# Windowed attention feeding a squared-ReLU MLP on one core: the first loads in another order, and the last quarter of W1 as two column halves

## The chip, the cores and the metric

The kernel runs on one core of one Trainium2 chip. The metric is the device time of one execution in microseconds (us). Three runs of the kernel before took 302.31, 302.37 and 302.68 us; the median is 302.37 us. Lower is better.

## What is computed

Eight batches of eight heads with 576 positions and 64 channels go through attention with a symmetric window of 32 positions. The result, laid out as 4608 tokens by 512 features, goes through a two-layer MLP.

```python
scores = (1/sqrt(64)) * q @ k^T              # per batch and head, 576 x 576
scores = where(|i - j| <= 32, scores, -1e9)
attn   = softmax(scores)
x      = (attn @ v) as [4608 tokens, 512]    # heads side by side
h      = x @ w_in                            # 512 -> 2048
out    = (relu(h) ** 2) @ w_out              # 2048 -> 512
```

Inputs and output are float32 in device memory; the products run in bf16 with float32 accumulation.

## The kernel before, in words

**Groups.** A group G is 192 tokens of one batch: three per batch, 24 in all (G = 3·batch + g). For each group, K and Q are brought to SBUF and turned so that the head channels lie on the partitions (`turn_pe` for batches 0 and 1, `turn_dma` later). Then `scores` (S) makes two windows A and B with matmuls, ScalarE takes the exponential, VectorE masks it, `pv` (P) multiplies with V, VectorE normalises into `xa` and `xb`, and `xturn` (T) turns the result into XT, the MLP's input. For the first three groups T runs on TensorE, later by DMA from the SP queue.

**MLP.** `mm1` makes h^T for some tokens: it is called At0.d below (first token t0, first of two blocks d of 128 hidden columns; for the first 768 tokens it is 8 matmuls of 192 columns). ScalarE applies relu (line 758), VectorE squares into GT (line 761). Two PSUM banks ht0 and ht1 take turns, and four relu buffers. A0.0 and A0.2 read the first quarter of W1, A0.4 and A0.6 the second, A0.8 and A0.10 the third, A0.12 and A0.14 the last. `mm2` is called Bu.seg: 128 output tokens u, a quarter seg of the hidden columns, 4 matmuls of 512 columns; it reads quarter seg of W2.

**Order of the work.** Every step is recorded with its engine, what it reads and writes, a duration and a key. `schedule` (lines 129 to 232) plays this through with a cost table and places the step with the smallest key among those ready; `emit` then writes one fixed instruction list for each engine, with semaphore waits. At run time each engine takes its list in order: a step whose input is late holds up all that stand behind it on that engine. Where TensorE has a gap in the plan, idle matmuls on zeros are put in (line 324).

**First loads.** Nearly all loads are issued from GpSimd (POOL): they cast float32 to bf16 and go through one software queue, in the order of `OPENING` (lines 71 to 74). K and Q of group 0 are the exception: `load_hw` (line 400) loads them as float32 from SP into a staging tile `oe`, and ScalarE and VectorE cast them. Below, "k3" is K of group 3, "v2.1" the second V tile of group 2, "w1.3" the last quarter of W1. In bf16 a quarter of W1 or W2 has 512 KB, a Q load 192 KB, K 224, 192 or 160 KB (g = 0, 1, 2), a V tile 64 to 128 KB. The kernel's order is: q2, v0.1, v0.0, k1, v1.0, q1, **w1.0**, k2, **w1.1**, v1.1, **w1.2, w1.3**, v2.0, v2.1, w2.0, q3, k4, k3, v5.0, w2.1, v4.1, w2.2, v3.0, q4, v4.0, v3.1, w2.3, v5.1, k5, q5.

**Regrouping.** `load_pair` (line 424) loads K and Q of batches 0 and 1 with two neighbouring positions in one row. For G < `NRAWP` (groups 0 to 2) `turn_pe` turns these rows as they lie, with 16 transposes into 64 output partitions each (line 499). For groups 3 to 5 a VectorE copy (line 439) first regroups the rows, and 8 transposes into 128 output partitions follow (line 501).

**Gates on later loads.** From group 6 on a load waits for an earlier step (`gate`, line 383): before group `GFAR` for the score or MLP step recorded last, from it on for the second P step (PB) of the group three before.

Of the kernel before, what the change touches and what calls it, by code (L numbers as in the profile page):

```python
# [18 lines left out]
RING = 1536  # L19
NV, NRAW = 6, 6  # L20
NTURN = 2
NRAWP = 3
TCOL = 200
NXT = 3
LEAD = 13.0
LAG = 9.0
AHEAD = 9.0
GFAR = 9
GATE = 'P{}B'
GD = 3  # L30
GK = 8.5
# [3 lines left out]
HMOVE = 27  # L35
PMOVE = 20
WMOVE = 81
VMOVE = 14.5
TISS = 1340
TMOVE = 15  # L40
# [8 lines left out]
VCS = 6  # L49
NDUP = 1  # L50
NPR = 4
LSLACK1 = 1000
HOLD = {'PE': 300}
KMIN = 0.5
HOLDT = 26000
KSPL = 0
XTD = 1
# [10 lines left out]
VSET = (-12, -9)  # L68
ESPLIT = 0
IOTA = -1  # L70
OPENING = [("q", 2), ("v", 0, 1), ("v", 0, 0), ("k", 1), ("v", 1, 0), ("q", 1), ("w1", 0), ("hq", 0), ("k", 2), ("w1", 1), ("v",
           1, 1), ("w1", 2), ("w1", 3), ("v", 2, 0), ("v", 2, 1), ("w2", 0), ("q", 3), ("hk", 0), ("k", 4), ("k", 3), ("v", 5, 0),
           ("w2", 1), ("v", 4, 1), ("w2", 2), ("v", 3, 0), ("q", 4), ("v", 4, 0), ("v", 3, 1), ("w2", 3), ("v", 5, 1), ("k", 5),
           ("q", 5)]
WARM = 40000
LAST = ((0, 256), (256, 384), (384, 512))
KC = ((0, 224), (224, 192), (416, 160))
# [196 lines left out]
def act(n):  # L274
    return 175 + 0.833 * n


def dve(n, fast=True):
    return 153 + (0.52 if fast else 1.04) * n


class Gen:
# [100 lines left out]
    def gate(self, G):  # L383
        if G < 6:
            return None
        return self.p.named[GATE.format(G - GD)] if G >= GFAR else self.moe

# [36 lines left out]
    def load_pair(self, t, b, g, key):  # L424
# [5 lines left out]
        s = (self.q if t == "q" else self.k)[b][:, t0:t0 + n, :].rearrange("h (p r) d -> p h (r d)", r=2)  # L430
        if G < NRAWP:
            self.p.rec("POOL", lambda e: e.dma_start(self.pairs(raw)[0:h].rearrange("p (h c) -> p h c", c=128), s),  # L432
# [4 lines left out]
                   dma=(f"{t}p{G % NPR}", G), key=key, dur=500 + 3 * h, move=(h // 2, PMOVE), name=f"{t}{b}{g}",  # L437
                   slack=LSLACK1 if b else 0)
        self.p.rec("DVE", lambda e: e.tensor_copy(raw[0:h, :, :].rearrange("p r (h d) -> p r h d", d=64),
# [4 lines left out]
    def load_v(self, b, g, key, js=(0, 1)):  # L444
        G = 3 * b + g
        vt = self.V[G % NV]
        for j in js:
            k0 = 192 * g - 32 + 128 * j
            lo, hi = max(k0, 0), min(k0 + 128, S_)
            if g and j == 0 and G < NVR:  # L450
# [3 lines left out]
                vt[lo - k0:hi - k0, j, :, 0:64], self.v[b, :, lo:hi, :].rearrange("h p d -> p h d")),  # L454
                writes=[("v", G % NV, j)], dma=(f"v{G % NV}{j}", G), key=key, dur=500 + 3 * n, move=(n // 2, VMOVE),
                name=f"v{b}{g}{j}", after=self.gate(3 * b + g), slack=LSLACK if b > 1 else LSLACK1 * b)

# [3 lines left out]
                   reads=[("v", (G - 1) % NV, 1)], writes=[("vl", G % NV)], key=key + VKEY, dur=300, name=f"vc{G}",  # L461
                   after=self.moe if G >= VCS else None)

    def load_w1(self, d, key):
        src = self.w_in[:, 512 * d:512 * d + 512].rearrange("(f p) c -> p f c", p=128)
        self.p.rec("POOL", lambda e: e.dma_start(self.W1[:, :, 512 * d:512 * d + 512], src),  # L466
                   writes=[("w1", d)], dma=(f"w1{d}", 0), key=key, dur=770, move=(32, WMOVE), name=f"w1{d}")

    def load_w2(self, d, key):
        src = self.w_out[512 * d:512 * d + 512, :].rearrange("(k p) c -> p k c", p=128)  # L470
        self.p.rec("POOL", lambda e: e.dma_start(self.W2[:, 4 * d:4 * d + 4, :], src),
                   writes=[("w2", d)], dma=(f"w2{d}", 0), key=key, dur=770, move=(32, WMOVE), name=f"w2{d}")

# [8 lines left out]
    def turn_pe(self, t, b, g, key):  # L482
# [9 lines left out]
        def f(e):  # L492
            for j in range(4):
                for x in range(2):
                    c = n * j + h * x
                    if G < NRAWP:
                        for u in range(2):
# [6 lines left out]
        self.p.rec("PE", f, reads=[("raw", t, G % NRAW, 0), ("raw", t, G % NRAW, 1), "id"], writes=tag, key=key,  # L504
                   dur=8 * 52 + TCOL * (G < NRAWP), name=f"turn{t}{b}{g}")
        if G < NPAIR:
# [233 lines left out]
    def mm1(self, t0, n, ds, key):  # L740
        k = self.k1
        self.k1 += 1
        ht, rt, gt = self.HT[k % 2], self.RT[k % 4], self.GT
        r = t0 % RING
        c = n * len(ds)
        d0 = ds[0]
        steps = [(t0 // 64 + x) % (RING // 64) for x in range(n // 64)]

        def f(e):
            for x, d in enumerate(ds):  # L750
                for ft in range(4):
                    mm = e.matmul(ht[:, n * x:n * x + n], self.W1[:, ft, 128 * d:128 * d + 128], self.XT[:, ft, r:r + n],  # L752
                                  start=(ft == 0), stop=(ft == 3))
            return mm

        self.moe = self.p.rec("PE", f, reads=[("xt", s) for s in steps] + [(("xt", s), 1) for s in steps if t0 < 192 and XTD] + [("w1", d0 // 4)], writes=[f"ht{k % 2}"], key=key,
                   dur=4 * len(ds) * max(n / 2.4 + 2.5, 33), name=f"A{t0}.{d0}")
        self.p.rec("ACT", lambda e: e.activation(rt[:, 0:c], ht[:, 0:c], ACTF.Relu), reads=[f"ht{k % 2}"],  # L758
                   writes=[("rt", k % 4)], key=key, dur=act(c), name=f"r{t0}.{d0}")
        rr = rt[:, 0:c].rearrange("p (d t) -> p d t", d=len(ds))  # L760
        self.p.rec("DVE", lambda e: e.tensor_tensor(gt[:, d0:d0 + len(ds), r:r + n], rr, rr, ALU.mult),  # L761
                   reads=[("rt", k % 4)], writes=[("gt", s, d) for s in steps for d in ds], key=key, dur=dve(c),
                   name=f"g{t0}.{d0}")
# [50 lines left out]
    def build(self):  # L814
        p = self.p
        self.k1 = 0
        self.moe = None
        K = -100.0
        self.setup_idle()
        self.setup_iota(K + IOTA)  # L820
        self.setup_id(K)
        self.setup_mask(2, K + 1)
        self.setup_bias(2, K + 1.1)
        self.setup_mask(1, K + 2)
        self.setup_bias(1, K + 2.1)
        self.setup_k(0, K + 0.5)
        self.setup_v(0, K + 1.5)
        self.setup_v(1, VSET[0])
        self.setup_v(2, VSET[1])
        self.setup_mask(0, MKEY[0])  # L830
        self.setup_mask(3, MKEY[1])
        for i in range(3, NV):
            self.setup_v(i, -9)
        self.setup_k(1, -9)
        for n, it in enumerate(self.opening()):
            kd, a = it[0], it[1:]
            key = K + n
            if kd == "w1":
                self.load_w1(a[0], key)
            elif kd == "w2":  # L840
                self.load_w2(a[0], key)
            elif kd == "v":
                self.load_v(*divmod(a[0], 3), key, a[1:])
            elif kd[0] == "h":
                self.load_hw(kd[1], a[0], key)
            else:
                self.load_pair(kd, *divmod(a[0], 3), key)
        for g in (1, 2, 4, 5):
            self.copy_v(g, K + 7 if g < 3 else 3 * g - LEAD - AHEAD)
        todo = []  # L850

        def at(key, f, *a):
            todo.append((key, len(todo), f, a))

        for G in range(NG):
            b, g = divmod(G, 3)
            if b > 1:
                key = 3 * G - LEAD - (GK if G >= GFAR else AHEAD)
                for t in "kq":
                    at(key, self.load_pair if G < NPAIR else self.load_qk, t, b, g, key)  # L860
                at(key, self.load_v, b, g, key)
                if g and G < NVR:
                    key = 3 * G - LEAD - 0.5 if G >= VCS else key
                    at(key + 0.01, self.copy_v, G, key - VKEY if G >= VCS else key)
            for t in "kq":
                key = 3 * G - LEAD - (0.6 if b < NTURN else TDKEY)
                at(key, self.turn_pe if b < NTURN else self.turn_dma, t, b, g, key)
            for ws in ((0,), (1,)) if G < NSPLIT else ((0, 1),):
                at(3 * G - LEAD + 0.3 * ws[0], self.scores, G, ws)
            for w in range(2):  # L870
                at(3 * G - LEAD + 0.3 * w + 0.1, self.pv, G, w)
            at(3 * G - LEAD + 0.5, self.xturn, G)
        t0 = 0
        while t0 < NTOK:
            n = FIRST[t0] if t0 in FIRST else 192 if t0 < 768 else 256 if t0 < T512 else 512
            m = min(512 // n, 4)
            for d in range(0, 16, m):
                key = t0 / 64 + d / 16 * n / 64
                at(key, self.mm1, t0, n, list(range(d, d + m)), key)
            t0 += n  # L880
        at(500, self.mm2_last, NBLK - 1, 500)
        for u in range(NBLK - 1):
            for seg in range(4):
                at(2 * u + LAG + seg * 0.5, self.mm2, u, seg, 2 * u + LAG + seg * 0.5)
        for key, _, f, a in sorted(todo, key=lambda x: x[:2]):
            f(*a)
        p.schedule()
        with self.nc.Block():
            dsems, dcount = p.emit()
            for s in dsems:  # L890
                if s[0] == "o":
                    self.nc.sync.wait_ge(dsems[s], dcount[s])

    def opening(self):
        return OPENING

# [31 lines left out]
```

## Time and profile before

| | us |
|---|---|
| median of three runs | 302.37 |
| the profiled execution's own time | 302.63 |
| its span, first to last instruction | 300.5 |
| TensorE busy | 291.0 (97 %) |
| VectorE busy | 164.8 (55 %) |
| ScalarE busy | 160.6 (53 %) |
| GpSimd busy (all of it issuing loads) | 106.9 (36 %) |
| granted TensorE clock | 1.00 in every stretch |

The profile is of one execution. TensorE's share counts the idle matmuls as busy. The time of a load is given from its issue to its landing, when its semaphore lets a waiting engine go on; loads of one queue overlap, so the distance between two landings is what one of them adds. A program on one core has one granted clock, and here it is 1.00 throughout.

### The profile page before, as it was taken

The page shows a single profiled execution, that of the slowest core. Times are in us where ns is not written, and L with a number is a line of the kernel's source. Part 1 is how long each engine was busy: PE and PEld are TensorE (multiplying, and loading weights), DVE is VectorE, ACT ScalarE, POOL GpSimd, SP SyncE. Part 2 cuts the span into 40 slices and gives each one's busy share as a digit, 9 for nine tenths or more (in the row PEclk, how much of TensorE's full clock was granted, in tenths as well). Part 3 has the DMA queues.
Part 4 walks back from the last instruction along what each step waited for, and adds up shares of the span by engine and source line. Part 5 has one row for each costly group of instructions (what it writes and reads, how often), then busy time and mean ns, then how long its engine had stood idle before and what let it go on. Part 6 is the DMA issues. An engine that isn't in the chain of part 4 may idle for free.

```text
span 300.5 us, 6284 instructions
## 1 busy us (share of the span) xinstructions
PE 291.0 (97%) x2431; PEld 170.5 (57%) x2469; DVE 164.8 (55%) x381; ACT 160.6 (53%) x250; POOL 106.9 (36%) x143
## 2 busy tenths in 40 slices
PE   7888999999999999999999999999999999999997
PEld 2567885857767777754444444444544544444445
DVE  6787586666775757652765666546557632222100
ACT  3775555846656746650766376536646643443312
POOL 8992065235543661365246235533500000000000
DMA  9999999998999999999999999999992110001012
GB/s 162 191 199 185 192 180 197 182 163 131 158 182 146 113 157 142 171 127 169 180 158 85 154 165 150 139 146 161 160 130 65 55 52 37 35 35 37 36 70 105
DMA packets 160636, 39.83 MB, mean 133 GB/s; under 512 B 149984, under 2 KB 156128, under 8 KB 160608
## 3 DMA queue, kind: packets, MB, share of 16 engines
q0 software_dynamic: 106016, 17.93, 86.6%
q1 hardware_dynamic: 49264, 12.14, 28.0%
q10 hardware_dynamic: 5328, 9.37, 10.0%
q8 instruction: 19, 0.31, 0.4%
q14 instruction: 9, 0.07, 0.1%
HBM read 36.70 MB, written 9.44 MB: 154 GB/s over the span
## 4 chain that ended last, share of the span: by engine, by line
PE 90%; DMA 5%; POOL 3%; issue 1%; ACT 0%; POOLq 0%
PE ht L752 41%; PE outp L772 40%; DMA w<-in_moe_w_in_dram 5%; PE at L580 4%; PE at L637 4%; POOL v L453 1%; POOL w L466 1%; PE at L501 1%; PE ht L797 1%; PE outp L797 1%; POOL qraw L432 1%; POOL kraw L432 0%; ACT rt L758 0%; ACT oe L782 0%; ACT oe L807 0%
## 5 line engine op out<-in xcount | busy, mean ns | idle before, releaser
L752 PE MATMUL ht<-xt,w 128*128 128x256 bf16 (+2 forms) x885 | 140.0, 302 | 1.9 <-DMA w<-in_moe_w_in_dram 1.1
L772 PE MATMUL outp<-w,gt 128*128 128x512 bf16 x534 | 133.4, 379 | 1.5 <-issue 0.2
L758 ACT ACTIVATE rt<-ht 128x512 bf16<-128x512 f32 (+1 forms) x152 | 85.7, 578 | 80.0 <-PE ht L752 75.9
L752 PEld LDWEIGHTS ht<-xt,w 128*128 128x128 bf16 x896 | 81.1, 98 | 44.5 <-ACT rt L758 1.1
L761 DVE TENSOR_TENSOR gt<-rt 128x512 bf16<-128x512 bf16 (+1 forms) x152 | 61.5, 409 | 67.2 <-ACT rt L758 65.6
L772 PEld LDWEIGHTS outp<-w,gt 128*128 128x128 bf16 x560 | 52.0, 98 | 54.8 <-ACT oe L782 1.3
L396 POOL DMA_DIRECT2D kraw<-in_k_dram x36 | 27.7, 778 | 108.0 <-issue 43.6
L604 ACT ACTIVATE e<-at 128x1024 bf16<-128x1024 f32 x46 | 44.8, 1022 | 12.4 <-PE at L580 12.2
L609 DVE TENSOR_TENSOR pt<-e,mask 128x1024 bf16<-128x1024 bf16 x46 | 31.7, 692 | 26.8 <-ACT e L604 26.6
L782 ACT ACTIVATE oe<-outp 128x512 f32<-128x512 f32 x35 | 20.9, 599 | 36.1 <-PE outp L772 36.1
L453 POOL DMA_DIRECT2D v<-in_v_dram x48 | 38.4, 815 | 0.0
L396 POOL DMA_DIRECT2D qraw<-in_q_dram x36 | 27.8, 780 | 0.0
L637 PEld LDWEIGHTS at<-v,pt 128*128 128x128 bf16 x384 | 18.1, 98 | 10.6 <-issue 1.7
L637 PE MATMUL at<-v,pt 128*128 128x65 bf16 x384 | 20.1, 194 | 1.2 <-DVE at L665 1.0
L659 DVE TENSOR_TENSOR xa<-at,rs 64x512 bf16<-64x512 f32 x24 | 16.7, 694 | 0.8
L659 DVE TENSOR_TENSOR xb<-at,rs 128x512 bf16<-128x512 f32 x24 | 16.6, 690 | 0.8
L580 PEld LDWEIGHTS at<-qt,kt 64*128 64x128 bf16 x384 | 10.8, 94 | 9.4 <-issue 5.9
L580 PE MATMUL at<-qt,kt 64*128 64x128 bf16 x384 | 15.2, 218 | 0.7 <-ACT e L604 0.5
L656 DVE RECIPROCAL rs<-at 64x8 f32<-64x8 f32 (+1 forms) x48 | 10.0, 209 | 10.4 <-PE at L637 8.7
L665 DVE MEMSET at<- 64x520 f32 x23 | 11.3, 492 | 3.6 <-DVE xa L659 2.7
L804 DVE COPY oe<-ht 128x128 f32<-128x128 f32 x1 | 0.3, 292 | 14.7 <-PE ht L797 14.7
L460 DVE COPY v<-v 64x512 bf16<-64x512 bf16 x16 | 5.5, 346 | 4.3 <-PE ht L752 3.2
(69 smaller groups left out, 78.0 us busy)
## 6 DMA issues: line engine op xcount, KB each, us to landing
out_dram<-oe ACTq DMA_DIRECT2D x35, 256.0 KB, 3.0
qraw<-in_q_dram POOLq DMA_DIRECT2D x36, 96.0 KB, 5.4
v<-in_v_dram POOLq DMA_DIRECT2D x16, 128.0 KB, 7.0
w<-in_moe_w_in_dram POOLq DMA_DIRECT2D x4, 512.0 KB, 11.1
w<-in_moe_w_out_dram POOLq DMA_DIRECT2D x4, 512.0 KB, 18.9
v<-in_v_dram POOLq DMA_DIRECT2D x16, 96.0 KB, 6.0
kraw<-in_k_dram POOLq DMA_DIRECT2D x12, 112.0 KB, 4.6
kraw<-in_k_dram POOLq DMA_DIRECT2D x12, 96.0 KB, 5.5
```

The costliest lines, as they stand in the source:

```text
L396: self.p.rec("POOL", lambda e, j=j: e.dma_start(raw[0:h, j, :].rearrange("p (h d) -> p h d", h=8), s[:, j]), writes=[("raw", t, G % NRAW, ...
L453: self.p.rec("POOL", lambda e, j=j, lo=lo, hi=hi, k0=k0: e.dma_start(vt[lo - k0:hi - k0, j, :, 0:64], self.v[b, :, lo:hi, :].rearrange("h ...
L580: mm = e.matmul(sc[:, 512 * par + 128 * j:512 * par + 128 * j + 128], kt[r:r + 64, j, k0:k0 + 128], q, start=G >= NBIAS, stop=True, skip_g ...
L604: self.p.rec("ACT", lambda e, e_=e_, sc=sc: e.activation(e_[:], sc, ACTF.Exp, scale=0.125), reads=tags[w], writes=[("e", n % 2)], key=key, ...
L609: self.p.rec("DVE", lambda e, pt=pt, ee=ee, mb=mb: e.tensor_tensor(pt[:], ee, mb, ALU.mult), reads=[("e", n % 2), ("mask", mi)], writes=[( ...
L637: mm = e.matmul(avp[:, c:c + 65], pt[:, 4 * (h % 2) + h // 2, :], vt[:, w, h, 0:65], start=(w == 0 and y == 0), stop=True, skip_group_chec ...
L659: self.p.rec("DVE", lambda e: e.tensor_tensor(x[r0:128, :].rearrange("p (x y c) -> p x y c", x=2, y=4), av[:, :, :, 0:64], rb, ALU.mult), ...
L752: mm = e.matmul(ht[:, n * x:n * x + n], self.W1[:, ft, 128 * d:128 * d + 128], self.XT[:, ft, r:r + n], start=(ft == 0), stop=(ft == 3))
L758: self.p.rec("ACT", lambda e: e.activation(rt[:, 0:c], ht[:, 0:c], ACTF.Relu), reads=[f"ht{k % 2}"], writes=[("rt", k % 4)], key=key, dur= ...
L761: self.p.rec("DVE", lambda e: e.tensor_tensor(gt[:, d0:d0 + len(ds), r:r + n], rr, rr, ALU.mult), reads=[("rt", k % 4)], writes=[("gt", s, ...
L772: mm = e.matmul(op[:], gt[:, d, r:r + 128], self.W2[:, d, :], start=(d == 0), stop=(d == 15))
L782: self.p.rec("ACT", lambda e: e.activation(oe, op[:], ACTF.Copy), reads=[f"outp{u % 2}"], writes=[("oe", u % 4)], key=key, dur=act(512), n ...
```

## The change

The constants, the list of first loads, and two functions are changed; three numbers (`TCOL`, `WHALF`, `LSLACK1`) and `HOLD` only feed the planner's table, and so act through the order that it writes.

```diff
-NRAWP = 3
-TCOL = 200
+NRAWP = 4
+TCOL = 100
-GFAR = 9
+GFAR = 10
+WHALF = 43
-LSLACK1 = 1000
-HOLD = {'PE': 300}
+LSLACK1 = 500
+HOLD = {}
-OPENING = [("q", 2), ("v", 0, 1), ("v", 0, 0), ("k", 1), ("v", 1, 0), ("q", 1), ("w1", 0), ("hq", 0), ("k", 2), ("w1", 1), ("v",
-           1, 1), ("w1", 2), ("w1", 3), ("v", 2, 0), ("v", 2, 1), ("w2", 0), ("q", 3), ("hk", 0), ("k", 4), ("k", 3), ("v", 5, 0),
-           ("w2", 1), ("v", 4, 1), ("w2", 2), ("v", 3, 0), ("q", 4), ("v", 4, 0), ("v", 3, 1), ("w2", 3), ("v", 5, 1), ("k", 5),
-           ("q", 5)]
+OPENING = [("v", 0, 0), ("q", 1), ("k", 1), ("k", 2), ("v", 0, 1), ("v", 1, 0), ("hk", 0), ("v", 1, 1), ("q", 2), ("w1", 0),
+           ("w1", 1), ("w1", 2), ("w1", 3, 0), ("w1", 3, 1), ("v", 2, 0), ("v", 4, 0), ("q", 3), ("v", 2, 1), ("k", 3), ("q", 4),
+           ("k", 4), ("v", 3, 0), ("w2", 0), ("w2", 1), ("v", 3, 1), ("w2", 2), ("q", 5), ("v", 5, 1), ("w2", 3), ("k", 5), ("v",
+           4, 1), ("hq", 0), ("v", 5, 0)]
-    def load_w1(self, d, key):
-        src = self.w_in[:, 512 * d:512 * d + 512].rearrange("(f p) c -> p f c", p=128)
-        self.p.rec("POOL", lambda e: e.dma_start(self.W1[:, :, 512 * d:512 * d + 512], src),
-                   writes=[("w1", d)], dma=(f"w1{d}", 0), key=key, dur=770, move=(32, WMOVE), name=f"w1{d}")
+    def load_w1(self, d, key, half=None):
+        c, n = (512 * d, 512) if half is None else (512 * d + 256 * half, 256)
+        src = self.w_in[:, c:c + n].rearrange("(f p) c -> p f c", p=128)
+        self.p.rec("POOL", lambda e: e.dma_start(self.W1[:, :, c:c + n], src),
+                   writes=[("w1", d, x) for x in ((0, 1) if half is None else (half,))], dma=(f"w1{c}", 0), key=key, dur=770,
+                   move=(32, WMOVE if half is None else WHALF), name=f"w1{d}" + ("" if half is None else f".{half}"))
...
-        self.moe = self.p.rec("PE", f, reads=[("xt", s) for s in steps] + [(("xt", s), 1) for s in steps if t0 < 192 and XTD] + [("w1", d0 // 4)], writes=[f"ht{k % 2}"], key=key,
+        self.moe = self.p.rec("PE", f, reads=[("xt", s) for s in steps] + [(("xt", s), 1) for s in steps if t0 < 192 and XTD] + [("w1", d0 // 4, x) for x in sorted({d // 2 % 2 for d in ds})], writes=[f"ht{k % 2}"], key=key,
```

What it does to the written lists, read from the two programs:

- **POOL.** Ahead of W1 stand now v0.0, q1, k1, k2, v0.1, v1.0, v1.1, q2; these are the same eight loads that stood ahead of w1.3 before, two of them (k2, v1.1) formerly between the quarters. Then w1.0, w1.1, w1.2 and the two halves w1.3a, w1.3b. After them: v2.0, v4.0, q3, v2.1, k3, q4, k4, v3.0, **w2.0, w2.1**, v3.1, **w2.2**, q5, v5.1, **w2.3**, k5, v4.1, v5.0. So w2.0 has eight loads between itself and W1, where it had two.
- **SP.** The staged K of group 0 is issued first and Q second; before, Q was first.
- **TensorE.** A0.12 waits for w1.3a alone and A0.14 for w1.3b alone. Ahead of A0.12 stand the same steps as before; P2A (V of group 2) stands behind A0.14 now, where it stood between the two. From there the list runs P2A, two A, turn q3, A, P2B, A, turn k3, A, T2, A, T2, two A, S3, two A, B0.0, P3A, B1.0, two A, B0.1, P3B, two A, B0.2, turns k4 and q4, two A, S4, B1.1, B0.3. Over the whole program it has the same instructions, but for 32 transposes of group 3 in place of 16 and one more idle matmul. The last 45 steps are the same.
- **VectorE.** The two regrouping copies of group 3 are gone.
- **ScalarE.** The copy of the first two feature blocks of XT for group 0 (line 700) stands behind the exponential of S1B, where it stood ahead of it.

More of the change, by code (lines that the diff above doesn't have):

```diff
@@ L838, in build @@
             if kd == "w1":
-                self.load_w1(a[0], key)
+                self.load_w1(a[0], key, *a[1:])
             elif kd == "w2":
```

## The prediction, made before the changed kernel had run

> **What bounds the kernel now.** I read the page first: TensorE (PE) is busy nearly all the time, and the chain that ended last is PE but for one DMA.
>
> ```profile
> PE 291.0 (97%) x2431; PEld 170.5 (57%) x2469; DVE 164.8 (55%) x381; ACT 160.6 (53%) x250; POOL 106.9 (36%) x143
> ...
> PE   7888999999999999999999999999999999999997
> ...
> PE 90%; DMA 5%; POOL 3%; issue 1%; ACT 0%; POOLq 0%
> ```
>
> PE is below nine tenths only in the first four slices (30 us) and the last. Then the chain of the first 50 us in order of time, which names the DMA:
>
> ```profile
> 8.48 0.89 POOL v L453
> 9.37 0.71 POOL w L466
> 10.08 14.15 DMA w<-in_moe_w_in_dram
> 24.23 0.14 issue
> 24.36 0.82 PE ht L752 x8
> 25.18 0.25 PE at L637 x8
> ```
>
> The load issued at 10.08 is w1.3, landing at 24.23. The TensorE timeline (start, length, operation, idle before it) shows who waits:
>
> ```profile
> 13.49 0.53 PE L499 MATMUL ht<-ident,qraw 96*64 96x96 bf16 x16
> ...
> 21.44 0.82 PE L752 MATMUL ht<-xt,w 128*128 128x192 bf16 x8 [0.19 <-DMA w<-in_moe_w_in_dram]
> ...
> 22.65 0.82 PE L752 MATMUL ht<-xt,w 128*128 128x192 bf16 x8
> 24.36 0.82 PE L752 MATMUL ht<-xt,w 128*128 128x192 bf16 x8 [0.89 <-DMA w<-in_moe_w_in_dram]
> ...
> 31.11 0.51 PE L501 MATMUL at<-ident,qraw 96*128 96x96 bf16 x8
> ```
>
> A0.8 starts at 21.44, when w1.2 has landed (21.33), and A0.12 at 24.36, after 0.89 us of idling for w1.3. From there on PE runs through: the table by stages has it 49.6 of 50 us busy between 50 and 100, and no wait after 26 us is longer than 0.2. So **the span is 24.36 us plus the PE work behind the gate, 276.1 us**. An edit counts if it moves the gate, moves work across it, adds PE work behind it, or opens a new gap there.
>
> **1. Landing of the last part of W1.** Landings, from the loads' issue rows (issue plus time to landing): q2 7.70, k1 10.15, q1 11.46, w1.0 13.82, k2 14.68, w1.1 17.90, v1.1 18.76, w1.2 21.33, w1.3 24.23. Is this issuing or moving? The table of one-microsecond stretches:
>
> ```profile
> 7.00:8.00 1.00, 0.53 (x17) 0.45 (x18) 0.81 (x8) 1.00 (x2) 1.00 (x2) 1.00 2.34 157
> 11.00:12.00 1.00, 1.00 (x26) 0.67 (x26) 0.96 (x2) 0.77 (x1) 1.00 (x2) 1.00 1.26 211
> 45.00:46.00 1.00, 0.94 (x14) 0.64 (x12) 0.88 (x2) 0.81 (x2) 0.00 (x0) 1.00 2.41 162
> ```
>
> The last two columns are the DMA share, over 1 throughout, and GB/s: 157 with K, Q, V alone, 211 with W1 alone. The engines are full, so the order matters little and the bytes ahead decide. Ahead of the end of W1 stand the same eight loads, four quarters and two staged loads as before. GpSimd needs 0.75 to 0.9 us per issue, so w1.3b is issued near 10.6, over 12 us ahead of its landing. Hence w1.2 lands at 21.3 again, w1.3a halfway, at 22.8, and w1.3b at 24.2 plus what shorter runs cost. Halves write runs of 512 B, quarters 1 KB; the trace has no 512 B runs. Bounds for 512 KB: 0, at the quarters' 211 GB/s; 0.8, at the 157 of K, Q, V (3.3 us against 2.5). Nearest are quarters with runs twice as long, so I take **+0.1: w1.3b at 24.3**. An earlier landing is also possible (rival 1).
>
> The Trainium skill ("DMA: Bandwidth & Descriptors", Specifications) has full rate from 512 B upwards, by which this term would be 0 and the sum 0.1 lower; no run here has such a load.
>
> **2. Work moved across the gate.** Ahead of it stand the same steps, plus A0.12, which needs w1.3a only. Eight 192-column matmuls take 0.66 us in the chain (16 in 1.32). In the old order A0.10 is done by 23.4, and w1.3a comes before that, so A0.12 fits before 24.3 and **0.66 us leave the tail**. What covers it: the opening must be 0.7 us ahead of the gate. It is rearranged: the copy L700 stands behind the exponential of S1B. By the rows (exponential 1.02, query copy 1.03) ScalarE does S1A's exponential, q2's copy, S1B's exponential, then L700 until about 17.0, against 14.9 before; A0.0 starts near 17.1, not 15.75. Then A0.0, A0.2, P1B, S2B, A0.4, A0.6 and T1 take 0.66 four times, 0.26, 0.33 and 0.42, to 20.8 with about 0.6 of waits: ahead of w1.2's 21.3. If the opening were 1 us later still, the gain would shrink by what exceeds the 0.7.
>
> **3. Group 3 without regrouping.** 16 transposes replace 8. In the chain, 8 take 0.34 (q) and 0.39 (k); 16 of the L499 kind take 0.46 (96 columns, 11.51 to 11.97, when the next starts) and 0.52 (112). So **+0.25 on PE**. The two VectorE copies (0.42 each) were not on the path: gain 0.
>
> **4. Loads behind W1.** These are new waits on PE, and all steps stand behind them. From 24.3 I add the distances between landings that like loads had before (V tiles 0.4 to 0.75, Q 1.15, k3 1.26, k4 1.07, a W2 quarter 2.6), and walk PE through its list with chain durations (A 0.66, B 0.86, P 0.26, S 0.55, T 0.22):
>
> | load | lands | PE is there |
> |---|---|---|
> | v2.0 | 24.7 | 25.1 |
> | q3 | 26.35 | 26.7 |
> | k3 | 28.15 | 28.7 |
> | w2.0 | 33.55 | 34.2 |
> | w2.1 | 36.15 | 37.5 |
> | w2.2 | 39.5 | 39.95 |
> | w2.3 | 43.8 | 44.2 |
>
> All in time, but by 0.35 to 0.65 in most rows; before, w2.0 landed at 27.47 for a B0.0 at 29.26. I take 0; rival 2 has the other end. Other covers: the evacuation of k3 waits on VectorE behind the regrouping of q4 (lands 29.4), but S3 is not due before 32.3. The first MLP step on DMA-turned tokens (A576.0, near 47.9) needs T3: issued near 39.6, 6.7 to landing as now, 46.3.
>
> **5. Smaller edits.** K before Q on SP: the two staged loads share 832 KB and end at 6.79 either way; S0 starts within 0.3 of its 9.39, which part 2's slack covers. The later gate of group 9 and the planner's constants only reorder a tail of the same steps; a switch between kinds of matmul shows up to 0.1 (16 A in 1.43 instead of 1.32 after S), and their number is 269 against 266: 0, with 0.3 either way.
>
> **Sum:** −0.66 + 0.25 + 0.1 = −0.31 us. The profiled execution took 302.63 (span 300.5 and 2.1 around it); it becomes 302.3, span 300.2. That execution is 0.26 above the median, so the forecast against 302.37 is **302.05 us**. A measurement of this kernel tells about 0.2 %, 0.6 us, from no change: my forecast lies inside.
>
> **Rivals.**
> - **1. W1 lands earlier.** Speaks for it: w1.1 came 3.2 and w1.3 2.9 us after the load ahead, while a quarter alone at 211 GB/s takes 2.5. If K, Q, V are through at 13.1 (1152 KB, at the pace that brought 864 KB by 11.46) and the W1 loads then follow at 2.55, w1.3b is there at 23.3. Against: the excess is that engines already move the next load (v2.0 and v2.1 land 0.4 and 0.8 after w1.3), which is not lost. PE would reach A0.14 at 23.5: −0.66 − 0.8 + 0.25 = −1.2, **301.2**. Chance 0.2.
> - **2. Slower: W2 comes late.** Eight loads now stand between W1 and w2.0, and w2.3's margin is 0.4 over 19.5 us of stream, so a stream 2 % slower than reckoned decides it. Mechanism: S3 and so T3 come earlier (near 32 and 36.6, not 36.3 and 41.8), and SP's transposing DMAs fall among w2.2 and w2.3; with them the rate falls to 162 (the last row above). At 173 GB/s, the mean of 41 to 46, the 3584 KB from v2.0 to w2.3 take 21.2 us, w2.3 lands 1.3 after PE gets there: **303.4**. Against: w2.3 itself came in 2.5 us beside the first of these. Chance 0.22.
> - **3. The split does nothing**, the opening being so late that A0.12 starts when w1.3b is there: −0.66 is gone, +0.35 stays, **302.7**. Chance 0.1.
> - **4. The second half pays a fixed time of its own.** v1.0 (64 KB) landed 0.46 after its forerunner and needs 0.39 at 167 GB/s, so a load adds 0.1 at most beyond its bytes: 302.15, inside the forecast, and its chance of more is 0.03. The Trainium skill ("DMA: Bandwidth & Descriptors", Anatomy of one DMA) has a fixed 2 us per DMA, mostly the receipt; were it paid in series, w1.3b would land 2 us late, 1.6 above the forecast. By that page, as by the trace, such times overlap where loads are queued.
>
> **Chances.** Forecast 0.45, own range 301.5 to 302.6 (parts 2 and 5 give 0.3 either way, part 1 up to 0.7 more): 0.12 of it beyond the 0.6 on the fast side, 0.33 within. Rival 1: 0.2, faster. Rival 2: 0.22, of which 0.03 within. Rivals 3 and 4: 0.13, 0.11 within. Faster 0.32, same 0.47, slower 0.21. Range: rival 1's time to most of rival 2's: 301.2 to 303.1.
>
> **What would show it.** Part 1: w1.3b landing between 24.1 and 24.6. Part 2: an A step running while w1.3b is in flight, and PE idle for a DMA once more ahead of A0.14. Part 3: L499 with 32 more matmuls near 27 and 29 us. Part 4: no PE wait for a DMA after that gate; a gap ahead of the first B on w2.0, w2.2 or w2.3, or of a turn of group 3, proves it wrong. A gate below 23.8 is rival 1. An idle stretch after 100 us that I did not name would be a failure of part 5.

## The result, and the profile after

The changed kernel took 304.43 us (median of six executions, 303.66 to 305.37); the kernel before, measured beside it, 302.52 (six, 302.25 to 303.46). The ratio is **1.0059, 95 % interval 1.0036 to 1.0083**: slower by 0.6 %. The forecast was 302.05, range 301.2 to 303.1, so the time lies outside the range, on the other side of no change. The profiled execution took 303.84, span 301.9 (before 302.63 and 300.5): 1.4 us of span to explain, of the 1.9 between the medians.

First the page of the changed kernel, the three lines that were shown of the kernel before:

```profile
PE 291.4 (97%) x2449; PEld 170.9 (57%) x2486; DVE 164.0 (54%) x379; ACT 161.3 (53%) x250; POOL 107.5 (36%) x144
...
PE   7888999998999999999999999999999999999996
...
PE 87%; DMA 8%; POOL 3%; issue 1%; ACT 0%; POOLq 0%; ACTq 0%
```

TensorE's busy time is the same (291.4 against 291.0). But there is an 8 among the nines, in the slice that begins at 67.9 us, and DMA's share of the chain has gone from 5 to 8 %. The chain up to 31 us, in order of time:

```profile
10.68 14.33 DMA w<-in_moe_w_in_dram
25.02 0.14 issue
25.15 0.82 PE ht L755 x8
...
29.69 0.52 PE at L502 x16
```

The DMA is w1.3b, issued at 10.68, landing at 25.02. Now TensorE's timeline, at the gate and at the 8 (start, length, operation, idle before it and what ended it):

```profile
23.49 0.82 PE L755 MATMUL ht<-xt,w 128*128 128x192 bf16 x8 [0.38 <-DMA w<-in_moe_w_in_dram]
25.15 0.82 PE L755 MATMUL ht<-xt,w 128*128 128x192 bf16 x8 [0.84 <-DMA w<-in_moe_w_in_dram]
...
68.64 1.03 PE L755 MATMUL ht<-xt,w 128*128 128x256 bf16 x8 [0.80 <-DMA xt<-xa]
```

A0.12 did run while w1.3b was in flight, as intended (23.49). But A0.14 then waited 0.84, and at 68.64 there is a wait that the kernel before does not have: A768.0, which reads 256 tokens, those of group 4 and the first of group 5, waits for the first half of T5, turned by DMA. For this pair of profiles the terms are: gate +0.79 (25.15 against 24.36), A0.12 moved ahead of it −0.66, the turns of group 3 +0.25 (their estimate), the new wait +0.80. That is 1.18 of the 1.4.

The wait at 68.64 is the visible end of something wider. The queue of SP, which issues the token transposes (T, lines 735 and 738) and those of K and Q (line 542); start, issue length:

```profile
41.11 1.77 SPq L738 DMA_TRANSPOSE xt<-xb  x1
49.27 1.18 SPq L735 DMA_TRANSPOSE xt<-xa  x1
50.50 1.30 SPq L542 DMA_TRANSPOSE kt<-kraw  x1
...
59.65 1.28 SPq L735 DMA_TRANSPOSE xt<-xa  x1
```

The first is the second half of T3. It landed 7.8 us after its issue, at 48.9, and A576.0, which needs it, started at 49.15, at once. In the kernel before the same tokens, issued at 44.51, landed 6.7 us later, at 51.2, for an A576.0 at 53.36. The two rows of before, then that of the changed kernel:

```profile
44.51 1.20 SPq L735 DMA_TRANSPOSE xt<-xb  x1
53.36 1.48 PE L752 MATMUL ht<-xt,w 128*128 128x192 bf16 x16
...
49.15 0.82 PE L755 MATMUL ht<-xt,w 128*128 128x192 bf16 x8
```

The last row of the SP queue above is the first half of T5: 8.9 us to landing, at 68.5. Between 49 and 62 us the transposes of the changed kernel took 7.1 to 8.9 us from issue to landing; before, 3.8 to 7.4. And the opening list of loads, with the same bytes, ended at 48.3, where it ended at 46.1. My reading of the reason, from the two traces side by side: T3's halves are issued at 38.14 and 41.11 (before 41.76 and 44.51) and the first load of group 6 at 34.52 (before 37.35), so 3 us more of that traffic falls among the last loads of the opening.

So the kernel before had 2.2 us of room ahead of A576.0 and 0.1 ahead of A768.0 (69.18, T5's first half landing at 69.1); the changed one has none ahead of either. In its written list A768.0 also stands ahead of P6A, B5.1 and B5.2, about 2 us of TensorE's work earlier.

### The profile page after: what moved, and what is told of

The parts are those of the page before. It is cut to its first block, busy times and chain, and to the rows that moved or that the text cites. A ratio compares the mean times of both kernels' runs of the same rounds, so it can differ in the third digit from the quotient of the medians.

```text
span 301.9 us, 6318 instructions
## 1 busy us (share of the span) xinstructions
PE 291.4 (97%) x2449; PEld 170.9 (57%) x2486; DVE 164.0 (54%) x379; ACT 161.3 (53%) x250; POOL 107.5 (36%) x144
## 4 chain that ended last, share of the span: by engine, by line
PE 87%; DMA 8%; POOL 3%; issue 1%; ACT 0%; POOLq 0%; ACTq 0%
PE ht L755 40%; PE outp L775 37%; DMA w<-in_moe_w_in_dram 5%; PE at L640 4%; PE at L583 4%; DMA xt<-xa 3%; POOL v L454 1%; POOL w L468 1%; PE ht L800 1%; PE outp L800 1%; POOL qraw L433 1%; POOL kraw L433 0%; PE at L504 0%; PE at L502 0%; ACT oe L810 0%
## 5 line engine op out<-in xcount | busy, mean ns | idle before, releaser
L755 PEld LDWEIGHTS ht<-xt,w 128*128 128x128 bf16 x896 | 81.2, 98 | 46.5 <-ACT rt L761 2.5
```

## The experiments

Every kernel below runs the written lists of the kernel it starts from (each engine's order, read from the recording) with only the edit shown. Ratios are to executions of the kernel before on the same chip, between those of the edited one. Of the theories that the expectations name, three run through several of them: **H**, the second half of the last quarter lands later than a whole quarter would, so that the split gains nothing at the gate; **X**, A768.0 has lost its room, and waits for T5; and from f1_v41_early on **V**, the late v4.1 holds VectorE. "Waits" are TensorE's idle times of over 0.2 us in the profiled execution, with the releaser that the timeline names.

**1. The changed kernel once more, and the halves undone and done alone.**

a1_after_again: no edit.

> The changed kernel once more, unaltered, beside the three that follow. Theory: its profile was 1.2 us slower than that of before by two terms, the last W1 load landing at 25.0 and not 24.2, and a wait of 0.8 us of the step A768.0 for the turned tokens of group 5; both are there again, and the median is near 304.4. Rival: the wait for the turned tokens is an accident of one execution; then it is absent or over 2 us in this profile.

Measured 304.04 us (six), ratio 1.0047 (1.0030 to 1.0063). The loss is there again. In this profile w1.3b landed at 24.72, the wait at 68 us is absent, and another of 0.89 stands at 81.43: the gate moves by 0.3, and the late wait by a whole step, from one execution to the next.

e1_whole_quarter:

```diff
-("w1", 3, 0), ("w1", 3, 1),
+("w1", 3),
```

> The changed kernel with the last quarter of W1 as one load again, every other instruction in the same place on every engine. Theory H (the halves make the end of W1 land late): the quarter lands at 24.2 to 24.4, A0.12 starts at 24.4 and A0.14 0.66 later, at 25.1, where the changed kernel has it: same time as the changed kernel within 0.2 us. Theory O (the new order of loads makes it late): it lands at 24.9 to 25.1, A0.14 starts at 25.8, and the kernel is 0.7 us slower than the changed one.

Measured 304.58, ratio 1.0053 (1.0034 to 1.0073). w1.3 landed at 23.92 (9.96 + 13.96), about 0.8 to 1.1 ahead of w1.3b in the two profiles with halves, and the time stayed where it was: halves seem to land later by what they save, as theory H has it. One later landing (g4_v41_whole, in experiment 7) goes against this, all nineteen together bear it out (part 1 below). The profiled execution is the slowest of the six, 305.40, and has three late waits: 0.44 at 49.32 for the second half of T3, 0.89 at 68.74 ahead of A768.0, 0.86 at 82.75.

e3_before_halves: the kernel before with the opposite edit.

> The kernel before with the last quarter of W1 as two column halves; the order of loads and of every engine's steps as before, so that A0.12 waits for the first half and A0.14, behind P2A, for the second. Theory H (halves land late): the second half lands near 25.0, A0.14 starts at 25.15, and since A0.12 and P2A (0.92 us in the chain) lie ahead of it the time is 0.1 us below before: no change. Theory O (the order of loads is at fault): the second half lands at 24.2 to 24.4, and the time falls by 0.8 to 0.9 us below before.

Measured 302.77, ratio 0.9994 (0.9983 to 1.0004): no change here either. The split neither gains nor costs anything that these runs can tell, in either order.

**2. Group 3 without regrouping, alone.** e4_before_turn, the kernel before with

```diff
-NRAWP = 3
+NRAWP = 4
```

> The kernel before with group 3 turned without regrouping, the only change: 32 transposes into 64 partitions in place of 16 into 128, and two VectorE copies less; the order of all steps as before. By the term of the prediction it is 0.25 us slower than before. Rival: the two copies that fall away free VectorE ahead of the evacuation of k3, and the time falls by up to 0.3.

Measured 303.05, ratio 1.0003 (0.9990 to 1.0015), that is +0.1 us, −0.3 to +0.45. The predicted +0.25 lies inside; so does nothing.

**3. More room ahead of A768.0.** e2_a768_later, the changed kernel with TensorE's list

```diff
-B5.0 A768.0 P6A A768.2 A768.4 B5.1 P6B ... B5.2
+B5.0 P6A B5.1 B5.2 A768.0 A768.2 A768.4 P6B
```

> The changed kernel with three TensorE steps (P6A, B5.1, B5.2: 0.26 + 0.86 + 0.86 us) ahead of A768.0 as the kernel before has them; no other engine's list changes. Theory X (the planner's new constants put A768.0 2 us too early for the turned tokens of group 5): the wait of 0.8 us is gone, nothing takes its place, and the median falls by 0.8 us or more below the changed kernel's, to 303.6 or less. Rival: the turned tokens and the scores that follow are late as a whole, so a wait of the same length opens at the next steps and the time stays within 0.3 of the changed kernel's.

Measured 304.44, ratio 1.0064 (1.0033 to 1.0094). The wait at 68 us is gone and nothing is won: 0.56 us opened at 50.33 and 0.29 at 81.03. The rival had it right. Its VectorE timeline showed a cause I had not had in view:

```profile
47.35 0.21 DVE L659 RECIPROCAL rs<-at 64x8 f32<-64x8 f32 x1 [0.18 <-PE at L640]
48.58 0.29 DVE L461 COPY v<-v 64x512 bf16<-64x512 bf16 x1 [1.03 <-DMA v<-in_v_dram]
48.90 0.69 DVE L662 TENSOR_TENSOR xa<-at,rs 64x512 bf16<-64x512 f32 x1
49.78 0.49 DVE L668 MEMSET at<- 64x520 f32 x1 [0.18 <-DVE xa L662]
```

VectorE stands 1.03 us at its copy of v4.1, which the changed kernel loads last but one. Behind that copy, on the same engine, stand the xa tile of group 4 (then T4 and, behind T4 on SP, the transposes of group 6) and the zeroing for P4B. The same idle time is 0.41 us in e1_whole_quarter and 0.77 in l1_after_light; in the profiles of the changed kernel itself the copy came just after the landing (47.98 against 47.43).

**4. Less traffic.** l1_after_light and l2_before_light, the changed kernel and the kernel before with

```diff
-e.dma_start(raw[0:h, j, :].rearrange("p (h d) -> p h d", h=8), s[:, j])
+e.dma_start(raw[0:h, j, :].rearrange("p (h d) -> p h d", h=8)[:, 0:nh], s[:, j, 0:nh])
```

where nh is 2 for groups 6 to 8, else 8. K and Q of the other six heads are left out there, so these groups' output is not the reference's.

> The changed kernel, but K and Q of groups 6, 7 and 8 are loaded for two of the eight heads only (the other heads keep older values, so the attention of these groups is not the reference's); every instruction stands in its place on every engine. That takes 0.88 MB out of the software queue between 35 and 70 us. Theory D (the load stream and the transposing DMAs of 40 to 85 us have become late, so PE waits 0.8 to 2.3 us there for turned tokens or V tiles, at steps that vary): these waits vanish, and the time falls by 0.8 us or more below the changed kernel's, to 303.2 or less. Rival P (the waits come from the order on PE, SP or VectorE, not from the load of the DMA engines): they stay, and so does the time within 0.3 us.

> The kernel before with the same loads of groups 6, 7 and 8 cut to two heads; everything else in its place. Its trace has no waits after 26 us. Theory D: the time stays within 0.5 us of the kernel before, and its distance to the changed kernel with the same cut is what the opening alone makes, 0 to +0.4 us, in place of 1 to 1.9. Rival P: the distance stays over 1 us.

Measured 303.68, ratio 1.0024 (1.0006 to 1.0042) for the changed kernel; 302.91, ratio 0.9998 (0.9987 to 1.0010) for the kernel before. Traffic that the old order carries for nothing costs the new one about half of its loss. The transposes between 49 and 62 us now took 3.4 to 6.4 us to landing, and no wait of TensorE stands behind 26 us in the profiled execution (303.07), though executions went up to 305.0.

**5. Does the kernel before have such waits?** b1_before_again: no edit, one execution with a profile.

> The kernel before once more, for a second trace. Theory D: it has no wait over 0.3 us after 26 us, or one much smaller than the changed kernel's. Rival: waits of 0.8 us between 40 and 85 us are there too, and the first trace was lucky.

It took 304.63 us, 1.2 over the slowest of its six beside the changed kernel, with two waits, 1.61 at 49.97 and 0.40 at 82.95. So the old order is not free of them, though in all later measurements none of its executions was over 304. Two of the edited versions that follow the old order show a late wait of over 0.5 us in their profiles, e3_before_halves (0.69 at 70.02) and g2_before_late_v41 (0.86 at 82.30); the profiles of before, e4_before_turn and l2_before_light have none behind 26 us. The longer one in b1_before_again has a cause of its own, told at the end.

**6. v4.1 early.** f1_v41_early, the changed kernel with the loads

```diff
-... w2.1, v3.1, w2.2, q5, v5.1, w2.3, k5, v4.1, v5.0
+... w2.1, v3.1, v4.1, w2.2, q5, v5.1, w2.3, k5, v5.0
```

> The changed kernel with one load moved: v4.1 goes out right behind v3.1, ahead of w2.2, where the changed kernel has it nearly last. All lists of all engines but the order of these loads stay. Theory V (the late v4.1 holds VectorE's copy, behind it the xa tiles and Z of group 4, and with them P4B and the token transposes): v4.1 lands near 37.6 us, VectorE has no idle time over 0.15 us that ends with a V tile between 40 and 50 us, and the time falls by 0.3 to 0.8 us, to about 303.6, a ratio near 1.002 to the kernel before. Rival (a v4.1 that is late is only a sign of a DMA stage that is full; the transposes of groups 3 and 5 are late for their own reason, with no room ahead of A576.0 and A768.0): the waits of TensorE at 49 and 68 to 69 us stay, and the time stays at 304.1 to 304.5, ratio 1.004 to 1.006.

Measured 303.46 (twelve), ratio **1.0020 (1.0002 to 1.0038)**: 0.6 us under a1_after_again, 1.0 under the first measurement, as theory V gave it. The interval still overlaps that of a1_after_again; g4_v41_whole against e1_whole_quarter, the same move with the whole quarter, repeats the gain (1.0017 against 1.0053) with intervals that do not meet. v4.1 landed at 37.8. The path that the theory named is not seen in this profile, though: the copy started at 48.38, no earlier, because VectorE had waited for another load:

```profile
47.09 0.42 DVE L440 COPY kraw<-kpair 80x1024 bf16<-80x1024 bf16 x1 [0.84 <-DMA kpair<-in_k_dram]
47.43 0.68 DVE L612 TENSOR_TENSOR pt<-e,mask 128x1024 bf16<-128x1024 bf16 x1
```

That is k5, landing at 47.1 (45.3 in the changed kernel), with v4.1 now ahead of it: over the profiles of the changed order k5 landed between 45.8 and 47.7 in the six with v4.1 early, and between 45.3 and 46.5 in the five with it late. TensorE then waits 0.29 at 50.18. The gain is measured; how it is made is not shown.

g2_before_late_v41, the reverse: in the kernel before v4.1 is the last load, and VectorE's copy stands where the changed kernel has it.

> The kernel before with v4.1 as the last load of its list and VectorE's copy of it moved to where the changed kernel has it, just ahead of the xa tile of step P4A; all else as before. Theory V: the copy waits for v4.1, which now ends the stream near 46 us (34.8 before), with 0.3 us or more of idle time on VectorE that ends with a V tile; but this order has some 2.3 us of room ahead of A576.0, so that little of it reaches TensorE: ratio 0.9995 to 1.002. If a late v4.1 is enough by itself: a wait of TensorE near 50 us and a ratio of 1.003 to 1.006. If it has nothing to do with it: no idle time on VectorE, ratio 0.999 to 1.0005.

Measured 303.29, ratio 1.0010 (0.9996 to 1.0025). v4.1 landed at 45.88, the copy was not held, and 0.86 us of waiting appeared at 82.30 in this profile. A late v4.1 by itself does not make the loss; what a held copy would do in this order the run does not test. (Its profiled execution also has a spell of half clock, told at the end.)

**7. The rest of f1.** Each edit is on top of f1_v41_early. f2_v41_a768 has also the edit of e2_a768_later; g5_v41_a576 gives A576.0 the room:

```diff
-B2.0 A576.0 P4B A576.2 ... A576.12 B2.1 P5A B2.2
+B2.0 B2.1 P4B B2.2 A576.0 A576.2 ... A576.12 P5A
```

> The changed kernel with v4.1 early as in f1_v41_early, and P6A, B5.1 and B5.2 ahead of A768.0 as in e2_a768_later. If the room ahead of A768.0 and the late v4.1 are both causes: no wait of TensorE between 49 and 69 us, time 302.9 to 303.4 (ratio 1.000 to 1.002). If the waits only move from step to step while the DMA engines are full (as in e2_a768_later, where they opened at 50 and 81 us): 304.1 to 304.5, and a wait appears elsewhere between 49 and 85 us.

> f1_v41_early with A576.0 behind P4B and two more steps of the second matmul (B2.1 and B2.2), so 2 us of work later, as far from its transposed tokens as in the kernel before. If the missing room ahead of A576.0 holds what is left: fewer slow executions (none over 304), median 302.9 to 303.2, ratio 0.9995 to 1.001. If the waits only go to another step (as in f2_v41_a768): ratio 1.002 or more, with a wait of TensorE between 50 and 85 us.

Measured 305.02, ratio 1.0067 (1.0050 to 1.0084), and 304.85, ratio 1.0059 (1.0041 to 1.0078): both give back all that v4.1 had won. The longest of TensorE's waits behind the gate in f2_v41_a768 (0.39 at 50.73 and 0.38 at 81.57 follow):

```profile
45.80 1.47 PE L775 MATMUL outp<-w,gt 128*128 128x512 bf16 x6 [0.98 <-DMA w<-in_moe_w_out_dram]
```

and g5_v41_a576:

```profile
57.59 0.41 PE L640 MATMUL at<-v,pt 128*128 128x65 bf16 x8 [0.51 <-DVE pt L612]
...
61.10 0.43 PE L640 MATMUL at<-v,pt 128*128 128x65 bf16 x8 [0.46 <-DVE at L668]
```

The first is B0.3 waiting for w2.3, in a step that the edit does not touch: in this execution the gate was 0.6 us earlier than in f1_v41_early (A0.14 at 24.36 against 24.97), and w2.3 was not (45.75 against 45.30). The second pair is the P steps behind the moved A576.0: ahead of the input of the first stand its relus on ScalarE, ahead of that of the second its squares on VectorE. So A768.0 and A576.0 are not short of room for want of a later place: what is put later there makes something else late. My reading of margins as the cause, in the form "give the step the room that it had", has fallen.

g4_v41_whole: w1.3 in one load.

> f1_v41_early with the last quarter of W1 as one load again. If the halves hold what is left: w1.3 lands near 23.9 to 24.2 us, A0.14 starts near 24.7 (24.97 in f1_v41_early), the time falls by 0.2 to 0.4 us, ratio 0.999 to 1.001. If they don't: ratio 1.001 to 1.003 as f1_v41_early.

Measured 303.28, ratio 1.0017 (1.0005 to 1.0030), as f1_v41_early. Its profile bears on the gate:

```profile
24.98 1.48 PE L755 MATMUL ht<-xt,w 128*128 128x192 bf16 x16 [1.93 <-DMA w<-in_moe_w_in_dram]
26.30 0.39 PE L640 MATMUL at<-v,pt 128*128 128x65 bf16 x7
```

A0.12 and A0.14 both stand behind the gate here, with 1.93 us of waiting, the full 0.66 later than in f1_v41_early; yet the span is the same 301.4. Step by step: the second output tile leaves at 48.98 against 48.40, 0.58 later, the third at 59.51 against 59.40. Of the 0.66 lost at the gate 0.1 is left by then, because f1_v41_early lost the rest near 50 us, and g4_v41_whole has no wait behind the gate. In the same profile the whole quarter landed at 24.84, where e1_whole_quarter with the same loads up to it had it at 23.92: one execution says little about when the end of W1 lands.

h1_v41_light: with the edit of l1_after_light.

> f1_v41_early with K and Q of groups 6, 7 and 8 loaded for two of the eight heads only (as in l1_after_light; the scores of these groups are left out for six heads). If what f1_v41_early still loses (0.2 %) is traffic: ratio 0.998 to 1.0005 and no slow executions as l1_after_light had. If it is a fixed cost (32 transposes instead of 16 for group 3 and the gate): ratio 1.001 to 1.0025 with no wait of TensorE behind 26 us.

Measured 303.66, ratio 1.0016 (1.0006 to 1.0025), all eleven executions between 302.83 and 304.06. Less traffic does not move the median, and the spread is no narrower than that of g4_v41_whole with all its traffic (303.06 to 304.09). I had expected either no loss or no wait; it has both, loss and waits:

```profile
24.43 0.82 PE L756 MATMUL ht<-xt,w 128*128 128x192 bf16 x8 [0.54 <-DMA w<-in_moe_w_in_dram]
45.59 1.90 PE L776 MATMUL outp<-w,gt 128*128 128x512 bf16 x8 [0.69 <-DMA w<-in_moe_w_out_dram]
50.77 0.43 PE L641 MATMUL at<-v,pt 128*128 128x65 bf16 x8 [0.64 <-DVE at L669]
```

The gate was early (24.43), and B0.3 at 45.59 and P4B at 50.77 took it back: B0.3 waits for w2.3, P4B for VectorE, which had stood 2.00 us for k5.

**8. The front alone, two attempts.** f5_before_front: the kernel before with the eight small loads ahead of all of W1. g6_v41_front: f1_v41_early with the old order of the loads up to the end of W1.

> The kernel before with the eight small loads ahead of W1 in the order of the changed kernel, W1 whole in four quarters behind them, and the rest of the loads in the order of the kernel before; all other lists are those of the kernel before. It isolates the front of the changed kernel from its order behind W1. If the front costs by itself (the end of W1 later by what the small loads ahead of it take): w1.3 lands 0.3 to 0.6 us later than in the kernel before and the time is 303.3 to 303.6, ratio 1.001 to 1.002. If only the order behind W1 costs: w1.3 at about the same place (24.0 to 24.3 us) and ratio 0.999 to 1.0005.

> f1_v41_early with the loads up to the end of W1 in the order of the kernel before (two quarters of W1 among the small loads; the last quarter still in halves). If the bytes ahead decide, as the prediction had it: w1.3b lands within 0.3 us of f1_v41_early's 24.83, and the ratio stays at 1.001 to 1.003. If the small loads ahead of all of W1 cost by themselves: w1.3b near 24.3 and a ratio near 1.000. If the order of TensorE's list, which was made for the small loads first, needs them: waits ahead of 20 us and a ratio over 1.003.

Measured 304.97, ratio 1.0056 (1.0038 to 1.0074), and 308.06, ratio 1.0174 (1.0152 to 1.0196). Neither isolates what it was made for: each pairs a front with a list of steps made for the other. VectorE or TensorE waits early on (in g6_v41_front 5.63 us at the copy of v1.1), and the granted clock falls to a half (below). The landings alone are of use: the last of W1 came at 24.7 in g6_v41_front against 24.8 in f1_v41_early, and at 24.3 in f5_before_front against 24.2 in the kernel before. The order of the loads ahead of the end of W1 moves it by no more than two profiles of one kernel differ, as the prediction had it.

**9. A faster kernel?** f3_before_room: the kernel before with the halves and with B5.3 ahead of A768.0.

> The kernel before with the last quarter of W1 in halves (as in e3_before_halves) and with B5.3 also ahead of A768.0, so that A768.0 has about 0.7 us more room than in the kernel before. If the room ahead of A768.0 costs the kernel before anything in its usual runs: 302.5, a ratio near 0.998, and no wait at 69 to 70 us. If it has room enough as it stands: the same as e3_before_halves, ratio 0.9985 to 1.0005.

Measured 303.14, ratio 0.9998 (0.9989 to 1.0006): the old order loses nothing there that these runs can tell. No version here beats the kernel before.

## Why the prediction was wrong, point by point

**What bounds the kernel.** "The span is 24.36 us plus the PE work behind the gate" was right for the kernel before and taken over for the changed one. There it fails. With the new order there is a second bound near 45 to 50 us, the end of the opening list of loads (w2.3, k5, v4.1, then T3 and T4), and a gate that is earlier or later by 0.6 us does not pass it (g4_v41_whole against f1_v41_early; h1_v41_light). Counted from A0.14's start, the prediction's terms leave 276.1 − 0.66 + 0.25 = 275.7 us. g4_v41_whole, gate at 25.64 and no wait behind it, has 275.8; f1_v41_early, gate at 24.97, has 276.4; the changed kernel, at 25.15, 276.8.

**Part 1, landing of the end of W1 (+0.1). This term was mis-sized.** 25.02 in the profile, 0.8 after w1.3 before. Over all nineteen profiles, both orders, the end of W1 landed at 23.8 to 24.8 as one quarter (eight, mean 24.1) and at 24.2 to 25.0 as halves (eleven, mean 24.7): the halves come 0.6 later, give or take 0.3, not 0.1. That is nearly the 0.66 that part 2 wins, and agrees with the times, which the split does not move (e1_whole_quarter, e3_before_halves, g4_v41_whole). Of the 0.56 that parts 1 and 2 were to gain together some 0.1 is left. Its upper bound of 0.8 was wide enough; the row from which "W1 alone" took its 211 GB/s still has q1 landing in it, at 11.46. By the page of the Trainium skill that the prediction named ("DMA: Bandwidth & Descriptors", Specifications) this term is 0, which these landings do not show; but a half differs from a quarter both in its runs and in being one load more, and no run here parts the two.

**Part 2, work across the gate (−0.66).** The mechanism is as described: A0.12 at 23.49, one more wait ahead of A0.14. The cover was also there, though the walk to 20.8 leaves out the 0.6 of waits that it names (17.1 and its steps make 20.75): T1 was through at 21.15, w1.2 landed at 21.5. The gain was spent by the later landing of part 1.

**Part 3, group 3 (+0.25).** 16 transposes took 0.46 and 0.52 in the chain, as costed, and the part alone measured +0.1 (−0.3 to +0.45). Right within what can be told.

**Part 4, loads behind W1 (0). This is the step that failed most.** With part 1 as measured the sum would have been near 302.5, or 0.05 % above the kernel before; the rest of the loss, 0.42 to 0.54 % by the two measurements, lies behind it. The table itself held: v2.0 25.5, q3 26.77, k3 28.60, w2.0 34.09, w2.2 39.46, w2.3 44.15, each 0.8 or less from the forecast, and TensorE waited for none of them. It stopped one load too soon and one step too soon. k5 and v4.1, at the end of the list, were in no row, because TensorE does not read them first; VectorE does, in order, ahead of things that TensorE and SP need. And "T3: issued near 39.6, 6.7 to landing as now" was 41.11 and 7.8 for the second half, so that the 1.6 us of room reckoned for A576.0 (46.3 against 47.9) were 0.2 (48.9 against 49.15). The time to landing had been carried over from the kernel before, where it was measured from 44.51 on and the list of loads ended at 46.1.

**Part 5 (0 ± 0.3).** The written order behind 45 us does more than "only reorder a tail of the same steps": A576.0 comes 4.2 us earlier (49.15 against 53.36), its tokens only 2.3 earlier (48.9 against 51.2).

**The rivals.** Rival 2 named this side, and its mechanism, T3's transposes among the last loads because S3 comes earlier, is what the SP queue shows. It placed the damage at w2.3; in the changed kernel it fell on T3 to T5 and the last loads, and on w2.3 as soon as v4.1 was moved ahead of it (f2_v41_a768, h1_v41_light). Its 303.4 was too little by 1. Rival 1 is out: no gate was near 23.3. Rival 3 is out as told, since A0.12 did run early; that the split wins nothing is true for another reason, the one of rival 4: with the same bytes the halves end 0.6 later, where rival 4 allowed 0.1 and gave more a chance of 0.03. Whether that is a fixed time or the shorter runs is open. (Rival 4's "1.6 above the forecast" is the distance to the kernel before, −0.66 + 0.25 + 2; to the forecast it is 1.9.)

**What is shown and what is open.** Of some 0.5 % (1.0047 and 1.0059), moving v4.1 takes back 0.25 to 0.4 %, and thinning the loads of groups 6 to 8 about as much; together they take back no more (1.0016). What remains, 0.2 %, shows in single profiles as waits for the end of the opening list (w2.3, k5) in h1_v41_light and as a later gate in g4_v41_whole, to which the turns of group 3 come; the runs don't divide it, and this share is read, not shown. Open is by which path the place of v4.1 acts: the copy is held in the profiles of three kernels (e1_whole_quarter, e2_a768_later, l1_after_light) and in neither of the two of the changed kernel itself. Not tried was to hold T3 or the loads of group 6 back until the opening list has ended, nor the later gate of group 9 (`GFAR`) alone.

## What to carry to other kernels

A gate that ends the longest wait is the bound only until the next one: before crediting work moved ahead of it, walk the consumers behind it up to the point where the DMA engines have room again, the ones on VectorE and SP too, since a load that a copy waits for holds all that stands behind the copy. An order that runs earlier also issues its own transfers earlier, into the stream that it depends on; a time to landing read from the old trace does not hold there. Where several loads end a full stream with no room, moving one ahead makes another late: compare whole orders, not steps.

## What the runs showed of the hardware that was not expected

- **Half clock after an early lull.** f5_before_front, stretches of 2 us (length, TensorE busy, granted clock, DMA share, GB/s):

```profile
12.00:14.00 2.00, 0.85 (x18) 1.00 1.38 203
14.00:16.00 2.00, 1.51 (x30) 0.69 1.24 208
16.00:18.00 2.00, 2.00 (x36) 0.50 1.24 203
...
22.00:24.00 2.00, 2.00 (x35) 1.00 1.86 175
```

  TensorE idled 1.64 us up to 14.49; the granted clock then was a half for about 6.8 us in all (the rows' shortfalls, 0.62, 1.00, 1.00 and 0.78 at 20 to 22, over one half), and 16 transposes took 0.85 us instead of 0.53. All six executions had a mean clock of 0.989 or 0.994. In g2_before_late_v41 an idle stretch of 1.20 us up to 8.07 was followed by 3.4 us of half clock (0.62 and 0.53 granted in the stretches 8 to 10 and 10 to 12), and in g6_v41_front the clock was a half for some 13.6 us from 13.6 on. The Trainium skill ("TensorE: Matmul & The Clock Gate", Part 1) halves the clock after a whole idle window of some 3.4 us and gives it back after a busy one. 3.4, 6.8 and 13.6 us are one, two and four such windows, which agrees; but ahead of them no idle stretch was longer than 1.64 us, so it takes less than a wholly idle window. In the opening an idle stretch under 2 us is thus not just its own length.
- **A store whose issue took 2.6 us.** In b1_before_again, ScalarE's first output store:

```profile
46.64 2.62 ACTq L787 DMA_DIRECT2D out_dram<-oe  x1
49.31 0.60 ACT L785 ACTIVATE oe<-outp 128x512 f32<-128x512 f32 x1 [2.70 <-PE outp L775]
```

  The next store there took 0.34, the first one in the profile of before 0.69. ScalarE stands still meanwhile, the next output tile is emptied late, and TensorE waited 1.61 us for its bank. The same, 2.81, stands in f5_before_front. What sets it off is open.
- **The same transpose took 2.6 or 7.6 us** from issue to landing (that of `xb` near 63 us, in l1_after_light and in the changed kernel). The two kernels differ only in the bytes loaded for groups 6 to 8.
